# Square roots through logarithm and exponential, and a score turn in two PSUM banks, in a fused attention and feed-forward kernel

## The chip, the cores and the metric

The kernel runs on one core of one Trainium2 chip. The metric is the device time of one execution in microseconds (us). The span of a profile is the stretch from the first to the last recorded instruction, some 2 us less than the device time of the same execution. PSUM is the on-chip memory in which TensorE's results land, SBUF the one that holds the operands.

## The reference, cut to what matters

```python
def _attn_ref(q, k, v, tau):              # B, N, C = 4, 6080, 256, fp32; tau = 1.0
    qn = q / (np.linalg.norm(q, axis=1, keepdims=True) + 1e-06)
    kn = k / (np.linalg.norm(k, axis=1, keepdims=True) + 1e-06)
    s = kn.transpose(0, 2, 1) @ qn / tau  # a 256 x 256 matrix for each batch
    s = s - s.max(-1, keepdims=True)
    a = np.exp(s)
    a /= a.sum(-1, keepdims=True) + 1e-09
    return v @ a

def _moe_ref(x, w_in, w_out, s, b):       # 24320 x 256 -> 2048 -> 256
    r = np.maximum(x @ w_in, 0.0)
    return (s * (r * r) + b) @ w_out
```

The norms run over the N rows, so each batch needs only 512 square roots: 256 for q, 256 for k. Everything else of weight is matrix products.

## The kernel before

For each batch the kernel forms the scores, turns them, exponentiates them, and multiplies the result into w_in ("wa"), so that the attention's own product with v disappears into the first feed-forward product. The first batch is done alone at the start. The finish of each of the other three is spread in small steps over the feed-forward of the batch before. These are the parts that the change touches:

```python
def add_norms(self, arrays=(0, 1), last=False):
    if self.b > 0:                        # later batches: sums of squares lie in the
        self.n_all = x_tile[0][:, 1, : 2 * CH].rearrange(...)   # unused half of X's bank
        self.n_ps = [self.n_all[:, 0], self.n_all[:, 1]]
    ...                                   # matmuls with a column of ones      (n_ps, o_ps<-ones,f)

def norms(a=None):                        # in finish_ops
    ...
    if a is None:                         # later batches: q and k together
        self.add_norms(last=True)
        po(nc.scalar.activation(out=st["nrm"], in_=self.n_all, func=AF.Sqrt))
    else:                                 # first batch: k, then q
        self.add_norms((a,), last=True)
        po(nc.scalar.activation(out=st["nrm"][:, a], in_=self.n_ps[a], func=AF.Sqrt))

def recip(a=None):
    ...
    po(nc.vector.tensor_scalar_add(out=nrm, in0=nrm, scalar1=EPS))
    po(nc.vector.reciprocal(out=r, in_=nrm))

def turn():                               # first batch: both halves in one PSUM bank
    st["t"] = self.bank("t_ps", CH, C)
    for ch in range(CH):
        for j in range(CH):
            po(nc.tensor.transpose(st["t"][:, j, ts(ch, P)], st["s"][:, ch, ts(j, P)], ident32))

def ready(func):                          # a tiny ACTIVATE that brings the table load early
    po(nc.scalar.activation(out=warm, in_=ones32[:, 0:1], func=func))

def exps(j):
    ...
    po(nc.scalar.activation(out=st["e"][:, j, :], in_=st["t"][:, j, :], func=AF.Exp,
                            scale=st["r"][:, 0, j : j + 1]))
# ... sums (r_ps, then rs = 1 / r_ps on VectorE), folds (wa_ps, scaled to wa by rs:
#     half 0 on ScalarE, half 1 on VectorE)

if self.b == 0:
    front = [lambda: norms(1), lambda: recip(1), lambda: norms(0),
             lambda: ready(AF.Exp), scale, lambda: recip(0), turn]
else:                                     # split and join: scores in two fp16 parts, turned by DMA
    front = [lambda: ready(AF.Sqrt), norms, recip]
    front += [lambda: ready(AF.Exp), lambda: split("hi"), lambda: split("lo"), join]
return front + [lambda: exps(0), lambda: exps(1), sums] + folds

# ... the end of the first batch, in program order
for f in fin[2:6]: f()
fin[6]()                                  # turn
transpose_v(0)                            # vT_ps x8, then the copy vT on VectorE
keep_busy(2, w_in16[:, 0, :P], w_in16[:, 0, :NW])   # two idle matmuls
for f in fin[7:13]: f()                   # exponentials, sums, first folds

# ... the second product of the feed-forward, a seven-product form (X, Y, Z: PSUM tiles)
def begin(name):
    t = ps_o.tile([P, 2, 2 * P], FP32, tag="o_ps", name="o_ps")
    halves = [t[:, h, :].rearrange("p (j c) -> p j c", j=2) for h in range(2)]
    if name == "X":
        st["X"] = halves[0]
        x_tile[0] = t                     # whose second half add_norms uses
    else:
        st["Z"], st["Y"] = halves
```

In the feed-forward, TensorE's h_ps matmuls (first product) alternate with o_ps matmuls (second product). ScalarE takes the relu of h_ps, VectorE squares and forms sums. An eviction is the copy of a result from PSUM to SBUF; that of wa_ps scales it too. An idle matmul is one whose result nobody reads.

## Time and profile before

| | kernel before |
|---|---|
| time, median of 3 runs | 719.26 us (719.24 to 719.51) |
| profiled span | 717.3 us |
| TensorE busy | 698.8 us |
| ScalarE busy | 544.7 us, of it 10.3 us in eight table loads |
| VectorE busy | 625.9 us |
| second h_ps matmul of the feed-forward | 39.19 us after the span's start |

Busy time adds up the instructions of an engine. It doesn't tell what a saving is worth: TensorE is the engine whose work fills the span, so a saving elsewhere counts only where TensorE was waiting for it. The last row matters because from about 40 us on TensorE runs nearly without a gap: the span after is the start of that stretch plus its length.

### The profile page before, as it was taken

To read this page: it belongs to the slowest core of one execution; us is meant where nothing else is said; L and a number is where in the kernel's file an instruction comes from. 1 tells how busy PE (TensorE), PEld (TensorE's weight loads), DVE (VectorE), ACT (ScalarE), POOL (GpSimd) and SP (SyncE) were. 2 spreads that over 40 slices of the span, in tenths; PEclk is the share of its full clock that TensorE was granted. 3 is DMA by queue.
4 is the path that set the end of the run, shared out by engine and by line. 5 is a ranking of instruction groups with operands and counts; after the bars stand their busy time and mean duration, and the time that the engine had idled before them with its cause. 6 is when DMAs were issued, how large, how long until landed. Compare 5 with 4: busy or idle time off the path is not lost.

```text
span 717.3 us, 17641 instructions
## 1 busy us (share of the span) xinstructions
PE 698.8 (97%) x7479; PEld 504.7 (70%) x7479; DVE 625.9 (87%) x881; ACT 544.7 (76%) x589; POOL 110.1 (15%) x189
## 2 busy tenths in 40 slices
PE   4799999999999999999999999999999999999998
PEld 3556777776677777777677777777668777777777
DVE  4879999998789999999889899999887888888886
ACT  4489977887777777788777778778877777777875
POOL 4532332101201222111110222110000000000000
PEclk9999999999999999999999999999999999999999
DMA  9999998646556879443982877944423333321201
GB/s 236 208 259 169 159 170 139 111 108 129 111 112 117 143 133 145 107 93 78 150 160 57 141 138 125 153 90 85 105 63 75 93 71 74 97 59 46 83 30 74
DMA packets 89790, 84.25 MB, mean 117 GB/s; under 512 B 59664, under 2 KB 64848, under 8 KB 89712
## 3 DMA queue, kind: packets, MB, share of 16 engines
q0 software_dynamic: 26064, 43.40, 37.2%
q1 hardware_dynamic: 63072, 38.43, 21.7%
q8 instruction: 58, 0.95, 0.6%
q10 hardware_dynamic: 576, 1.31, 0.5%
q14 instruction: 20, 0.16, 0.1%
HBM read 78.91 MB, written 24.90 MB: 145 GB/s over the span
## 4 chain that ended last, share of the span: by engine, by line
PE 93%; DMA 3%; DVE 2%; ACT 1%; POOL 1%; issue 0%; POOLq 0%; DVEq 0%; ACTq 0%
PE h_ps L636 45%; PE o_ps L804 40%; PE s_ps L146 4%; DMA qk<-in_q_dram 3%; PE wa_ps L323 2%; PE o_ps L708 1%; POOL qk L130 1%; PE o_ps L682 0%; ACT r L646 0%; DVE f L182 0%; DVE sq L166 0%; DVE o_sb L664 0%; DVE S L732 0%; DVE S L730 0%; DVE S L734 0%
## 5 line engine op out<-in xcount | busy, mean ns | idle before, releaser
L646 ACT ACTIVATE r<-h_ps 128x1024 f16<-128x1024 f32 (+1 forms) x384 | 387.9, 1014 | 146.0 <-PE h_ps L636 144.0
L636 PE MATMUL h_ps<-vT,wa 128*128 128x512 f16 (+7 forms) x1632 | 452.2, 364 | 0.1
L804 PEld LDWEIGHTS <-S 128*128 128x128 f16 x2944 | 198.0, 98 | 84.7 <-issue 0.2
L804 PEld LDWEIGHTS <-g 128*128 128x128 f16 x2208 | 155.0, 98 | 74.1
L659 DVE TENSOR_TENSOR g<-r 128x2048 f16<-128x2048 f16 (+2 forms) x150 | 174.7, 1164 | 14.6 <-ACT r L646 14.5
L804 PE MATMUL o_ps<-T,S 128*128 128x128 f16 x2208 | 183.3, 219 | 0.1
L636 PEld LDWEIGHTS <-wa 128*128 128x128 f16 x1632 | 136.1, 98 | 20.8 <-DVE wa L318 0.6
L804 PE MATMUL o_ps<-w_out,g 128*128 128x128 f16 x1472 | 134.2, 219 | 0.2 <-DVE u L664 0.2
L664 DVE SCALAR_TENSOR_TENSOR o_sb<-o_ps,s_out,u 128x256 f32<-128x256 f32 x138 | 66.4, 481 | 47.7 <-PE o_ps L804 45.2
L657 ACT ACTIVATE g<-r 128x1024 f16<-128x1024 f16 (+1 forms) x97 | 100.3, 1035 | 0.2
L146 PE MATMUL s_ps<-qk 128*128 128x256 f16 (+1 forms) x384 | 69.6, 282 | 13.9 <-ACT qk L137 8.8
L376 POOL DMA_DIRECT2D v<-in_v_dram x48 | 31.4, 654 | 263.0 <-DMA vT<-v 198.9
L664 DVE SCALAR_TENSOR_TENSOR u<-o_ps,s_out,rowconst 128x256 f32<-128x256 f32 x138 | 65.8, 477 | 0.0
L804 PE MATMUL o_ps<-w_out,S 128*128 128x128 f16 x736 | 63.4, 219 | 0.0
L804 PE MATMUL o_ps<-N,g 128*128 128x128 f16 x736 | 63.4, 219 | 0.0
L193 POOL DMA_DIRECT2D f<-f x30 | 26.4, 879 | 225.1 <-DVE f L182 171.9
L169 ACT ACTIVATE sq<-qk 128x1024 f16<-128x1024 f16 (+3 forms) x49 | 50.4, 1033 | 10.0 <-DMA qk<-in_k_dram 7.6
L732 DVE TENSOR_TENSOR S<-S,g 128x2048 f16<-128x2048 f16 (+1 forms) x47 | 56.4, 1201 | 1.3
L730 DVE TENSOR_TENSOR S<-g 128x2048 f16<-128x2048 f16 (+1 forms) x47 | 56.0, 1193 | 0.0
L734 DVE TENSOR_TENSOR S<-g 128x2048 f16<-128x2048 f16 x46 | 55.9, 1215 | 0.0
L736 DVE TENSOR_TENSOR S<-g,S 128x2048 f16<-128x2048 f16 x46 | 55.9, 1215 | 0.0
L146 PEld LDWEIGHTS <-qk 128*128 128x128 f16 (+1 forms) x384 | 32.8, 101 | 20.0 <-issue 7.9
(75 smaller groups left out, 323.7 us busy)
## 6 DMA issues: line engine op xcount, KB each, us to landing
out_dram<-o_sb SPq DMA_DIRECT2D x46, 512.0 KB, 3.0
v<-in_v_dram POOLq DMA_DIRECT2D x47, 256.0 KB, 4.7
qk<-in_k_dram POOLq DMA_DIRECT2D x42, 256.0 KB, 5.9
qk<-in_q_dram POOLq DMA_DIRECT2D x42, 256.0 KB, 7.1
f<-f POOLq DMA_DIRECT2D x30, 128.0 KB, 3.0
vT<-v SPq DMA_TRANSPOSE x182, 3.2
w<-in_moe_w_out_dram POOLq DMA_DIRECT2D x4, 512.0 KB, 11.4
raw<-in_q_dram ACTq DMA_DIRECT2D x2, 512.0 KB, 6.8
```

What stands on the lines that cost most here:

```text
L146: po(nc.tensor.matmul(self.s_ps[:, ch, :], kc[:np_, j, ts(ch, P)], qc[:np_, j, :], start=(c == 0 and j == 0 and ch == 0), stop=(c == len(s ...
L169: po(nc.scalar.activation(out=st["sq"][:np_, 1, js, :], in_=kc[:np_, js, :], func=AF.Square))
L636: po(nc.tensor.matmul(dst, wa[:, ci, ts(m, P)], src, start=(ci == 0), stop=(ci == CH - 1), skip_group_check=True))
L646: po(nc.scalar.activation(out=r16[:, :, i % 2, :n], in_=h_tiles.pop((g, i))[:, :, :n], func=AF.Relu))
L657: po(nc.scalar.activation(out=dst, in_=src, func=AF.Square))
L659: po(nc.vector.tensor_mul(dst, src, src))
L664: po(nc.vector.scalar_tensor_tensor(out=dst, in0=src, scalar=s_out, op0=ALU.mult, in1=add, op1=ALU.add))
L730: po(nc.vector.tensor_add(T[1], A21, A22))
L732: po(nc.vector.tensor_sub(T[2], T[1], A11))
L734: po(nc.vector.tensor_sub(T[3], A11, A21))
L736: po(nc.vector.tensor_sub(T[4], A12, T[2]))
L804: po(nc.tensor.matmul(st[name][:, j, :], a()[:, i, ts(j, P)], w[:, i, :], start=first, stop=last, skip_group_check=True))
```

## The change

The intent is that all of ScalarE's functions share one activation table. The square root becomes exp(ln(x)/2), the table is loaded once at the start, and the tiny warm-ups go. Besides, the turned scores of the first batch go to two PSUM banks, so that the first exponential needn't wait for the transposes of the second half.

```diff
+            def root(out, sums):
+                po(nc.scalar.activation(out=out, in_=sums, func=AF.Ln, bias=tiny))
+                po(nc.scalar.activation(out=out, in_=out, func=AF.Exp, scale=0.5))
...
-                    po(nc.scalar.activation(out=st["nrm"], in_=self.n_all, func=AF.Sqrt))
+                    root(st["nrm"], self.n_all)
...
-                    po(nc.scalar.activation(out=st["nrm"][:, a], in_=self.n_ps[a], func=AF.Sqrt))
+                    root(st["nrm"][:, a], self.n_ps[a])
...
             def turn():
-                st["t"] = self.bank("t_ps", CH, C)
+                st["t"] = [h_tile("t_ps")[:, 0, :C], self.bank("t_ps", CH, C)[:, 0, :]]
...
-            def ready(func):
-                po(nc.scalar.activation(out=warm, in_=ones32[:, 0:1], func=func))
...
-                         lambda: ready(AF.Exp), scale, lambda: recip(0), turn]
+                         scale, lambda: recip(0), turn]
             else:
-                front = [lambda: ready(AF.Sqrt), norms, recip]
-                front += [lambda: ready(AF.Exp), lambda: split("hi"), lambda: split("lo"), join]
+                front = [norms, recip]
+                front += [lambda: split("hi"), lambda: split("lo"), join]
...
-    warm = consts.tile([P, 1], FP32)
-    po(nc.scalar.activation(out=warm, in_=ones32[:, 0:1], func=AF.Sqrt))
+    po(nc.scalar.preload_act_table_set("natural_log_exp_and_others"))
+    tiny = consts.tile([P, 1], FP32)
+    nc.vector.memset(tiny, 1e-30)
...
-    FIN = (-12, 0, 3, 3, 5, 7, 15, 17, 19, 22)
+    FIN = (0, 3, 5, 7, 15, 17, 19, 22)
```

The cuts ("...") leave out unchanged lines and index changes that follow from the two shorter lists.

More of the change, by code (lines that the diff above doesn't have):

```diff
@@ L278, in join @@
             def join():
-                st["t"] = sm_pool.tile([P, CH, C], FP32, tag="sm_s", name="t_sb")
-                po(nc.vector.tensor_add(st["t"], st["hiT"], st["loT"]))
+                t_sb = sm_pool.tile([P, CH, C], FP32, tag="sm_s", name="t_sb")
+                po(nc.vector.tensor_add(t_sb, st["hiT"], st["loT"]))
+                st["t"] = [t_sb[:, j, :] for j in range(CH)]
             def turn():
-                st["t"] = self.bank("t_ps", CH, C)
+                st["t"] = [h_tile("t_ps")[:, 0, :C], self.bank("t_ps", CH, C)[:, 0, :]]
                 for ch in range(CH):
@@ L286, in turn @@
                         po(nc.tensor.transpose(
-                            st["t"][:, j, ts(ch, P)], st["s"][:, ch, ts(j, P)], ident32))
-            def ready(func):
-                po(nc.scalar.activation(out=warm, in_=ones32[:, 0:1], func=func))
+                            st["t"][j][:, ts(ch, P)], st["s"][:, ch, ts(j, P)], ident32))
             def exps(j):
@@ L296, in exps @@
                 po(nc.scalar.activation(
-                    out=st["e"][:, j, :], in_=st["t"][:, j, :], func=AF.Exp,
+                    out=st["e"][:, j, :], in_=st["t"][j], func=AF.Exp,
                     scale=st["r"][:, 0, j : j + 1]))
@@ L490 @@
             g0.mm(c, j)
-    for f in fin[2:6]:
+    for f in fin[2:5]:
         f()
-    fin[6]()
+    fin[5]()
     transpose_v(0)
     keep_busy(2, w_in16[:, 0, :P], w_in16[:, 0, :NW])
-    for f in fin[7:13]:
+    for f in fin[6:12]:
         f()
@@ L545, in at_step @@
         side.setdefault(int(s), []).append(f)
-    FIN = (-12, 0, 3, 3, 5, 7, 15, 17, 19, 22)
+    FIN = (0, 3, 5, 7, 15, 17, 19, 22)
     first_group = [b * N // TG for b in range(B)]
     FOLDS = (0, 0, 3, 4, 7, 8)
-    for i, f in enumerate(fin[13:]):
+    for i, f in enumerate(fin[12:]):
         at_step(FOLDS[i], f)
@@ L601, in fin_step @@
             for i, f in enumerate(ops):
-                at_step(int(s) + 1 + (FIN[i] if i < 10 else FIN[9] + 3 + (i - 10) * 3), f)
+                at_step(int(s) + 1 + (FIN[i] if i < 8 else FIN[7] + 3 + (i - 8) * 3), f)
         at_step(w1 - fin_len - 12, fin_step)
```

## The prediction

> **What bounds the kernel now.** I read the page's busy table first, then the chain that ended last, then ScalarE's groups with their shapes kept apart, and last the timelines and the chain in two short stretches.
>
> ```profile
> PE 698.8 (97%) x7479; PEld 504.7 (70%) x7479; DVE 625.9 (87%) x881; ACT 544.7 (76%) x589; POOL 110.1 (15%) x189
> ...
> PE 93%; DMA 3%; DVE 2%; ACT 1%; POOL 1%; issue 0%; POOLq 0%; DVEq 0%; ACTq 0%
> ```
>
> The reader is to see that TensorE is busy 97% of the span and is 93% of the chain that set the end, while ScalarE (ACT) is only 1% of that chain. From 40 us to 700 us TensorE has nearly no idle time. ScalarE time removed there is worth only what TensorE was waiting for. The next view is the list of ScalarE's groups; its columns are busy us, mean ns of one, and idle time before it.
>
> ```profile
> L646 ACT ACTIVATE r<-h_ps 128x1024 f16<-128x1024 f32 x376 | 383.1, 1023 | 143.1 <-PE h_ps L636 141.1 <-DVE S L736 1.2
> L291 ACT ACT_TABLE_LOAD x7 | 9.0, 1283 | 0.1
> L291 ACT ACTIVATE warm<-ones 128x1 f32<-128x1 f32 x7 | 1.4, 203 | 0.1
> L240 ACT ACTIVATE nrm<-o_ps 128x4 f32<-128x4 f32 x3 | 0.5, 174 | 0.0
> L243 ACT ACTIVATE nrm<-n_ps 128x2 f32<-128x2 f32 x2 | 0.3, 172 | 1.9 <-PE n_ps L224 1.9
> ```
>
> ScalarE waits 141 us for TensorE before its relus, so it has room. The seven loads and seven tiny warm-ups are 9.0 + 1.4 = 10.4 us in all. An eighth load stands at 1.18 us, under the first DMAs, and costs nothing: ScalarE then waits 3.31 us for its first rows.
>
> **What the Trainium skill says.** "ScalarE: Activation LUTs", section "What ACT_TABLE_LOAD costs", gives about 1283 ns for a load and about 1380 ns for a drain, 2.66 us a switch. The trace agrees on 1283 ns but shows no such drain: the root ends at 35.40, the load starts at 35.42, ends at 36.70, and the next ACTIVATE starts at 36.72. So I count 1.28 us plus 0.20 us of warm-up for a switch, not 2.66. The same section adds about 93 ns for a per-partition pointer operand; I use it for the new bias of the Ln: estimate 0.17 + 0.09 = 0.26 us. The same page, "Table sets: the hidden batching unit", says that natural_log_exp_and_others holds exp and ln and that cheap functions are in every set. The built program agrees as far as it can: one table load stands in ScalarE's stream in place of eight. "PSUM — Partial Sum Buffer", section "PSUM bank collisions raise a hardware error", tells to guard PSUM by bank; that is why the first exponential in the old layout, one bank for both halves, waits for all four transposes. No wait of this trace shows it, since the load hid it.
>
> **Instruction order.** Setting line numbers and buffer numbers aside, PE, POOL and SP run the same list before and after. VectorE gains one memset. ScalarE loses seven loads and eight warm-ups and has each Sqrt replaced by Ln and Exp, of which the second waits for the first. So all effects are of timing.
>
> **Part 1: the end of the first batch (34 to 40 us).** Here ScalarE is on the path.
>
> ```profile
> 35.01 0.20 PE n_ps L224 x8
> 35.21 0.02 issue
> 35.23 0.17 ACT nrm L243
> 35.40 0.02 issue
> 35.42 0.83 ACT L291
> 36.25 0.46 issue
> 36.72 0.20 ACT warm L291
> 36.92 0.74 ACT eT L296 x2
> 37.66 0.04 issue
> 37.70 0.23 PE r_ps L306 x3
> 37.93 0.90 PE wa_ps L323 x8
> ```
>
> This is the chain in order of time (start, us, what): root, table load, warm-up, two exponentials, then TensorE. It looks as if 1.28 + 0.20 us would come out. It does not, as the timelines of VectorE and TensorE beside it show (start, us, engine, line, operation):
>
> ```profile
> 34.00 0.73 DVE L166 TENSOR_TENSOR sq<-qk 128x512 f16<-128x512 f16 x2
> 35.05 0.88 DVE L257 TENSOR_SCALAR sm_s<-s_ps,rnrm 128x256 f32<-128x256 f32 x2 [0.32 <-PE s_ps L146]
> 35.84 0.16 DVE L248 TENSOR_SCALAR nrm<-nrm 128x2 f32<-128x2 f32 x1
> 36.04 0.17 DVE L249 RECIPROCAL rnrm<-nrm 128x2 f32<-128x2 f32 x1
> 37.21 0.69 DVE L389 COPY vT<-vT_ps 128x1024 f16<-128x1024 f16 x1 [1.00 <-PE vT_ps L387]
> ...
> 37.01 0.59 PE L462 MATMUL idle_ps<-w_in 128*128 128x512 f16 x2
> 37.44 0.49 PE L306 MATMUL r_ps<-parts,eT 128*128 128x1 f16 x4
> ```
>
> Step by step. A root now takes 0.26 + 0.03 (handing over, as between L248 and L249) + 0.20 = 0.49 us against 0.17: 0.32 longer. The root of k's sums (33.51) so moves the squares of q from 34.00 to 34.31; they end at 35.04 instead of 34.73. The last n_ps matmuls want the second of them: TensorE came to these at about 34.92, and now must wait to about 35.07, so they end 0.15 later, at 35.34. The root of q's sums then runs 35.38 to 35.87. VectorE does not reach its add before 35.84 anyway (the scaling of the scores stands ahead), so the reciprocal is done at 36.26 instead of 36.21. The third transpose ends at about 36.26. The first exponential can start at about 36.3 instead of 36.83: 0.5 us won, the rest of the load having hidden VectorE's work. The two end at about 37.15 instead of 37.66.
>
> But TensorE has eight transposes of v and two idle matmuls ahead of the r_ps matmuls. At about 216 ns each (the chain's 0.43 us for two 512-wide matmuls) the idle ones hold the array until 37.01 + 0.43 = 37.44, exactly where the first r_ps matmul stands. That one is not moved. What goes is the wait of 0.27 us for the second exponential at 37.70. So wa_ps starts at about 37.55 instead of 37.79: **0.25 us**. Behind it, ScalarE's first eviction also wants VectorE's reciprocal, which follows the vT copy that ends at 37.90 either way; it gains only about 0.1 us. VectorE's eviction (38.65) waits for wa_ps alone and moves by 0.25, and the second h_ps matmul at 39.19 waits for that one. So 0.2 to 0.25 us reaches TensorE's stream, and I see no transfer after it that would take it back. The two-bank turn adds to it only if the reciprocal is earlier than the fourth transpose (about 36.42): at most 0.1 us, hidden under the idle matmuls.
>
> **Part 2: the three later batches.** Each loses two loads and two warm-ups, 2 x (1.28 + 0.20) = 2.97 us, and gains 0.32 us: net 2.65 us of ScalarE, 7.9 us over three batches. How much TensorE waited for it is in the chain just after a load (load at 137.34 to 138.62, then two relus back to back from 138.75):
>
> ```profile
> 139.55 0.39 PE o_ps L804 x7
> 139.94 0.45 PE h_ps L636 x2
> 140.40 0.45 PE o_ps L804 x7
> 140.84 0.43 PE h_ps L636 x2
> ```
>
> 0.45 and 0.45 stand where the pattern is 0.43 and 0.39: 0.08 us lost. At the other five loads the distance of two h_ps pairs is 0.84 or 0.85 against 0.82: 0.02 to 0.03 each. The sum is about **0.2 us**. The longer root (0.49 at 147.64) fits before the relu at 148.15, which had waited 0.34 us for TensorE; the added 0.32 just fits.
>
> **Part 3: the start.** The table load now stands ahead of both of ScalarE's DMA issues, and the first moves from 0.74 by about 0.07 us. The second was issued at 1.25 while the load ran (1.18 to 2.46), so issue does not wait for a load. TensorE waits for data again later: estimate 0.
>
> Sum: 0.25 + 0.2 = 0.45 us of 719.26, that is 718.8 us.
>
> **The rivals.** (a) The full cost of the switches leaves the path: 7 x 1.48 = 10.4 us, 709 us, 1.4% faster, still inside 2%. Against it: ScalarE is 1% of the chain, and TensorE's list of waits holds none for a relu. (b) The longer serial root takes the load's place: k's root delays the squares, n_ps, q's root and the reciprocal by more than I reckon, and nothing or less than nothing is won at 36 us: 719.2 to 719.5. For it: 0.32 us twice in one chain. Against it: 0.5 us of margin up to 36.83. (c) The table load at the head delays the first q rows by 1.28 us: the first matmul at 7.08 goes to 8.4. Even then TensorE waits for rows near 23 and 28 us, so most is absorbed: up to 719.8. Against it: the second issue at 1.25.
>
> **Range and chances.** Runs of the kernel before lie within 0.27 us. My steps are off by perhaps 0.3 us at the first batch and 0.2 later, and small changes of timing move DMA waits at the start: 718.0 to 719.5. A change over 2% is 14.4 us, more than all the switches together; it would take a fault to make it slower by that.
>
> **What would show it right or wrong.** One load in ScalarE's groups. The first exponential at about 36.3, r_ps still at 37.44, wa_ps at about 37.55, the second h_ps matmul at about 38.95. Pairs of h_ps at 0.82 us throughout what was 137 to 141 us. The span shorter by about 0.45 us, half of it there by 40 us. If wa_ps does not move, (b) holds; if the first matmul comes after 8 us, (c). I would be wrong by more if the changed start reorders DMA landings before 33 us, or if the relu after the double root comes late.

## More of the kernel before

Every run quoted here was correct against the reference, with a granted TensorE clock of 0.999 or 1.0.

What the text calls a bank of PSUM is one whole o_ps tile of this program (2 x 256 fp32 for each partition).

## The result

| | before | after |
|---|---|---|
| median of 6 runs each, same rounds | 719.27 us (719.13 to 719.51) | 719.16 us (718.81 to 719.40) |
| ratio | | 0.9998, 95% interval 0.9985 to 1.001 |
| profiled span | 717.3 us | 717.2 us |
| second h_ps matmul | 39.19 us | 38.82 us |
| last matmul ends | 714.13 us | 713.96 us |

A ratio is the mean time of one kernel's fast runs over that of the other's of the same rounds, so not quite the ratio of the medians quoted.

The time lies inside the predicted range, but the gain is 0.1 us and not the predicted 0.45. The page's first part, for the kernel after (busy time, share of span and number of instructions of each engine), shows what was certain:

```profile
PE 698.9 (97%) x7479; PEld 504.6 (70%) x7479; DVE 626.1 (87%) x882; ACT 536.5 (75%) x579; POOL 109.8 (15%) x189
```

ScalarE lost 8.2 us of busy time (544.7 to 536.5), and TensorE's busy time stayed. The groups of ScalarE with shapes kept apart (busy us, mean ns of one, idle before) show the parts, for the kernel after:

```profile
L419 ACT ACT_TABLE_LOAD x1 | 1.3, 1283 | 0.7 <-PEq L882 0.7
...
L235 ACT ACTIVATE nrm<-o_ps,tiny 128x4 f32<-128x4 f32 x3 | 0.8, 264 | 0.0
L236 ACT ACTIVATE nrm<-nrm 128x4 f32<-128x4 f32 x3 | 0.6, 205 | 0.1
```

One load is left of eight. A later root is 264 + 205 ns where the Sqrt was 174 ns. Those 8.2 us mostly became idle time: ScalarE's idle time ahead of its relus rose from 146.0 to 153.4 us.

**The first batch.** This is the chain of waits of the kernel after, in order of time (start, us, what):

```profile
28.78 7.72 DMA v<-in_v_dram
...
36.55 0.62 PE vT_ps L390 x8
37.17 0.43 PE idle_ps L467 x2
37.60 0.08 PE r_ps L309 x4
37.68 0.90 PE wa_ps L326 x8
```

ScalarE is gone from this stretch of the chain. Before, it went through the root, the load, the warm-up and the two exponentials; now it comes from the arrival of v, through its transposes and the two idle matmuls, to r_ps and wa_ps without a wait. The timelines of ScalarE, VectorE and TensorE's weight loads (PEld) of the kernel after (start, us, engine, line, operation) show the ends of the side chains:

```profile
36.43 0.84 ACT L299 ACTIVATE eT<-t_ps,rnrm 128x256 f16<-128x256 f32 x2 [0.50 <-PE t_ps L293]
38.07 0.84 ACT L319 ACTIVATE wa<-wa_ps,rs 128x256 f16<-128x256 f32 x2 [0.80 <-DVE rs L314]
...
37.81 0.16 DVE L314 RECIPROCAL rs<-r_ps 128x2 f32<-128x2 f32 x1
38.18 0.92 DVE L321 TENSOR_SCALAR wa<-wa_ps,rs 128x256 f16<-128x256 f32 x2 [0.20 <-PE wa_ps L326]
...
38.59 0.21 PEld L641 LDWEIGHTS <-wa 128*128 128x128 f16 x2 [0.30 <-ACT wa L319]
```

The first exponential starts at 36.43 instead of 36.83, wa_ps at 37.54 instead of 37.79, and VectorE's eviction of wa_ps at 38.18 instead of 38.65. The second h_ps matmul is 0.37 us earlier.

The chain above names only one of the paths to the h_ps matmuls. The first of them waits for ScalarE's eviction (38.07 instead of 38.23), that eviction for the reciprocal rs on VectorE (37.81), and the reciprocal stands behind the copy of vT, which VectorE runs from 37.20 to 37.90 (records of VectorE overlap by some 0.08 us). So the first h_ps matmul gained 0.16 us (38.76 to 38.60). The second, which waited for VectorE's eviction before, stood 0.43 us behind the first and now stands 0.22 us behind it.

**After it.** TensorE's instruction list is the same in both kernels, so each matmul can be set against its twin. I took the start of each matmul minus the start of its twin in the kernel before, and took off the same difference at the second h_ps matmul. What remains is the lag that TensorE has gathered since: +0.19 us at the last matmul in the profile of the result, +0.26 in a second one of the same program. A second profile of the kernel before gives 0.00 to 0.01 throughout, so the method is good to 0.01 us. The lag comes in steps. The first is at the root of the second batch. Timelines of ScalarE and TensorE, kernel before:

```profile
147.64 0.17 ACT L240 ACTIVATE nrm<-o_ps 128x4 f32<-128x4 f32 x1
...
147.46 0.59 PE L636 MATMUL h_ps<-vT,wa 128*128 128x512 f16 x2
147.89 0.50 PE L804 MATMUL o_ps<-T,S 128*128 128x128 f16 x6
```

The same lines of the kernel after:

```profile
147.27 0.26 ACT L235 ACTIVATE nrm<-o_ps,tiny 128x4 f32<-128x4 f32 x1
147.56 0.20 ACT L236 ACTIVATE nrm<-nrm 128x4 f32<-128x4 f32 x1
...
147.09 0.59 PE L641 MATMUL h_ps<-vT,wa 128*128 128x512 f16 x2
147.58 0.50 PE L809 MATMUL o_ps<-T,S 128*128 128x128 f16 x6
```

From the start of the h_ps pair to the next o_ps matmul it was 0.43 us, which is the pair's own time; now it is 0.49. That o_ps matmul writes X, and the sums of squares that the Ln reads lie in the other half of X's PSUM bank. The Ln ends at 147.53 and the matmul starts at 147.58. Without a wait it would have started at 147.09 + 0.43 = 147.52.

The second step is at about 163.6 us, where both profiles of the kernel after have one and those of before have none. VectorE joins the two turned parts of the scores there. Its timeline before:

```profile
160.65 0.69 DVE L280 TENSOR_TENSOR t_sb<-t_hi,t_lo 128x512 f32<-128x512 f16 x1
```

And after:

```profile
161.09 0.69 DVE L285 TENSOR_TENSOR t_sb<-t_hi,t_lo 128x512 f32<-128x512 f16 x1 [0.72 <-DMA t_lo<-s_lo]
```

VectorE now waits 0.72 us for the last DMA transpose of the scores (0.81 us in the second profile). That transpose took 3.7 us from issue to landing before and 4.6 us after. TensorE lost 0.10 and 0.19 us shortly behind it, and the timelines show how: VectorE's later work moves with the join. Its read of X (u, L669) ran from 162.83 to 163.31, and the o_ps matmul that writes X next starts at 163.37, 0.17 us after the matmul ahead of it. Before, that read ended at 162.88, and the same matmul started at 163.59, 0.05 us after the one ahead. In the second profile the read ends at 163.71 and the matmul starts at 163.76.

### The profile page after: what moved, and what is told of

It is laid out like the page before. It is cut to its first block, busy times and chain, and to the rows that moved or that the text cites. A ratio compares the mean times of both kernels' runs of the same rounds, so it can differ in the third digit from the quotient of the medians.

```text
span 717.2 us, 17629 instructions
## 1 busy us (share of the span) xinstructions
PE 698.9 (97%) x7479; PEld 504.6 (70%) x7479; DVE 626.1 (87%) x882; ACT 536.5 (75%) x579; POOL 109.8 (15%) x189
## 4 chain that ended last, share of the span: by engine, by line
PE 93%; DMA 4%; DVE 1%; ACT 1%; POOL 1%; issue 0%; POOLq 0%; ACTq 0%
PE h_ps L641 45%; PE o_ps L809 40%; PE s_ps L146 4%; DMA qk<-in_q_dram 3%; PE wa_ps L326 2%; DMA v<-in_v_dram 1%; PE o_ps L713 1%; PE o_ps L687 0%; POOL qk L130 0%; ACT r L651 0%; DVE o_sb L669 0%; DVE S L737 0%; DVE sq L166 0%; DVE S L735 0%; DVE S L739 0%
## 5 line engine op out<-in xcount | busy, mean ns | idle before, releaser
L651 ACT ACTIVATE r<-h_ps 128x1024 f16<-128x1024 f32 (+1 forms) x384 | 388.4, 1014 | 153.4 <-PE h_ps L641 150.9
L669 DVE SCALAR_TENSOR_TENSOR o_sb<-o_ps,s_out,u 128x256 f32<-128x256 f32 x138 | 66.5, 482 | 47.1 <-PE o_ps L809 44.5
L669 DVE SCALAR_TENSOR_TENSOR u<-o_ps,s_out,rowconst 128x256 f32<-128x256 f32 x138 | 66.0, 478 | 0.0
```

The source lines that it names most:

```text
L651: po(nc.scalar.activation(out=r16[:, :, i % 2, :n], in_=h_tiles.pop((g, i))[:, :, :n], func=AF.Relu))
L669: po(nc.vector.scalar_tensor_tensor(out=dst, in0=src, scalar=s_out, op0=ALU.mult, in1=add, op1=ALU.add))
```

## The experiments

Twelve kernels ran, in five rounds each (e10 has six executions), on two chips. All outputs are right. The theory at this point: (A) the longer read of the root holds X's bank and delays TensorE, three times; (B) the former table loads were worth little in the later batches; (C) the first batch is set by v and not by the exponentials any more. The rivals: the two banks did the work or the harm at the first batch; the loads had been worth all the gain and a change of timing lost it again; the late DMA transpose is the whole loss.

The differences sought are tenths of a microsecond. The intervals of the times are about 0.12% wide to each side, 0.9 us, so **the times alone can't separate them**; the traces can, because TensorE's list is fixed. This table holds both. "v to h" is the time from the first transpose of v to the second h_ps matmul. The lag columns are TensorE's, in us, as above: just behind the first later root, behind the join near 163.6, behind the third root, and at the last matmul. Runs without the idle matmuls, or with v turned earlier, have other matmuls at the start; there the matching ones were compared.

| run | v to h | root 1 | join | root 3 | end | median us | ratio to before (95%) |
|---|---|---|---|---|---|---|---|
| before | 2.64 | – | – | – | – | 719.26 | – |
| e0_before_again | 2.63 | 0.00 | 0.00 | 0.00 | 0.00 | 719.42 | 0.9996 (0.9982 to 1.001) |
| after | 2.27 | +0.06 | +0.14 | +0.21 | +0.19 | 719.16 | 0.9998 (0.9985 to 1.001) |
| e0_after_again | 2.28 | +0.05 | +0.22 | +0.28 | +0.26 | 719.19 | 0.9996 (0.9984 to 1.0009) |
| e1_one_bank | 2.28 | +0.04 | +0.02 | +0.09 | +0.07 | 719.12 | 0.9998 (0.9986 to 1.0011) |
| e2_no_bias | 2.28 | 0.00 | -0.02 | -0.07 | -0.09 | 718.93 | 0.9988 (0.9976 to 1.0001) |
| e3_ln_twice | 2.28 | +0.35 | +0.34 | +1.00 | +0.98 | 720.08 | 1.0003 (0.999 to 1.0015) |
| e4_first_only | 2.28 | -0.02 | -0.02 | -0.02 | -0.02 | 718.61 | 0.9991 (0.9978 to 1.0003) |
| e5_later_only | 2.47 | +0.05 | +0.03 | +0.09 | +0.08 | 719.15 | 0.9999 (0.9985 to 1.0013) |
| e6_no_idle | 2.27 | +0.06 | +0.04 | +0.12 | +0.10 | 719.23 | 0.9995 (0.9983 to 1.0008) |
| e8_v_early | (3.43) | -0.01 | -0.02 | -0.07 | -0.09 | 718.47 | 0.9981 (0.9968 to 0.9995) |
| e9_join_later | 2.27 | +0.06 | +0.04 | +0.11 | +0.09 | 719.29 | 0.9993 (0.9979 to 1.0006) |
| e10_direct_no_idle | 2.28 | 0.00 | -0.02 | -0.06 | -0.08 | 718.93 | 0.9987 (0.9975 to 1.0) |
| e11_v_early_join | (3.40) | -0.01 | -0.02 | -0.07 | -0.09 | 718.67 | 0.9984 (0.9971 to 0.9996) |

In e8 and e11 the transposes of v no longer stand directly ahead of the sums, so "v to h" isn't comparable there. The kernel before ran again: 719.32 us beside e0_after_again, e1, e4 and e5; 719.61 us beside the others, on the second chip. Single executions of 720.0 to 720.6 us occur with several kernels, the one before among them; five of them have a span of 717.3 to 717.5 us like the others, so that their excess lies outside the profiled span.

### Both kernels again

e0_after_again and e0_before_again are the two kernels without an edit, for another profile of each.

> The changed kernel once more, to see what repeats. Theory A (the lead of 0.38 us won at the first batch is partly given back: 0.06 to 0.07 us at each of the three roots of a later batch because Ln with its bias pointer, 0.26 us, holds the PSUM bank longer than Sqrt, 0.17 us; another 0.11 us at 163.6 us by a late DMA transpose, by chance): the second h_ps matmul at 38.8 again, the three losses again, the loss at 163.6 not necessarily. Rival B (the differences after 40 us are scatter of single executions): the losses stand elsewhere or are missing. Time 719.1 us, within 0.3 us of before.

> The kernel before once more, for the scatter of its trace. If the arrival of the last q rows and of v sets when the first batch ends, its second h_ps matmul moves with them by up to 0.3 us from 39.19, while the rest of TensorE's stream keeps its distance from that matmul within 0.03 us. The late transpose (3.7 us to landing in the first profile) lands in 3.6 to 3.7 us and costs nothing if the late landings belong to the kernels without the later loads; in 4 us or more if it is chance. Time 719.3 to 719.6.

The lag repeats in the kernel after and is absent in the kernel before. The late transpose of the kernel before landed after 3.9 us this time, between the two cases of its expectation. What doesn't repeat is the absolute position. The first transpose of v stands at 36.55 in one profile of before and at 36.93 in the other, and at 36.55 and 36.86 in those of after, with all that follows moved by as much. The arrival of the first batch's rows moves the whole execution by up to 0.4 us, and that is as large as the effect in question.

### One bank for the turned scores

```diff
-                st["t"] = [h_tile("t_ps")[:, 0, :C], self.bank("t_ps", CH, C)[:, 0, :]]
+                t_ps = self.bank("t_ps", CH, C)
+                st["t"] = [t_ps[:, j, :] for j in range(CH)]
```

> The changed kernel with the turned scores of the first batch in one PSUM bank again. Theory A: both layouts wait for about the fourth transpose (36.42) or for the reciprocal (36.34), and the first r_ps matmul stands behind the idle matmuls at 37.44 in any case: the first exponential at 36.43 to 36.5, r_ps at 37.44, the second h_ps at 38.8, time unchanged (719.1). Rival: the two banks are worth something: the first exponential later by 0.1 us or more and the second h_ps matmul after 38.9.

"v to h" is 2.28 us with one bank and 2.27 or 2.28 with two. The first exponential starts 1.41 us after VectorE's first scaling of the scores with one bank, and 1.42 and 1.30 us after it in the two profiles with two banks; it is 1.30 in e2, e3, e4, e6 and e9 too. The third transpose ends 1.26 us and the fourth 1.37 us after the scaling, so that the exponential wins up to 0.11 us by the two banks. That stays hidden; at the h_ps matmul they are worth nothing that these traces can show.

### Only the first batch, only the later ones

e4_first_only has the new root and the two banks in the first batch and the Sqrt with its loads in the later ones. e5_later_only is the reverse, with one bank.

```diff
 # e4: later batches as before
-                    root(st["nrm"], self.n_all)
+                    po(nc.scalar.activation(out=st["nrm"], in_=self.n_all, func=AF.Sqrt))
-                front = [norms, recip]
-                front += [lambda: split("hi"), lambda: split("lo"), join]
+                front = [lambda: ready(AF.Sqrt), norms, recip]
+                front += [lambda: ready(AF.Exp), lambda: split("hi"), lambda: split("lo"), join]
-    FIN = (0, 3, 5, 7, 15, 17, 19, 22)
+    FIN = (-12, 0, 3, 3, 5, 7, 15, 17, 19, 22)
```

```diff
 # e5: first batch as before
-                    root(st["nrm"][:, a], self.n_ps[a])
+                    po(nc.scalar.activation(out=st["nrm"][:, a], in_=self.n_ps[a], func=AF.Sqrt))
-                         scale, lambda: recip(0), turn]
+                         ready, scale, lambda: recip(0), turn]   # loads the shared table, warm Exp
-    po(nc.scalar.preload_act_table_set("natural_log_exp_and_others"))
+    po(nc.scalar.activation(out=warm, in_=ones32[:, 0:1], func=AF.Sqrt))
```

> Ln and Exp, two banks and no table load in the first batch only; the later batches take Sqrt with two table loads each, as before. Theory A: the second h_ps matmul at 38.8, and the lead of 0.38 us over before is kept to the end, as nothing differs later: time 718.9 us, 0.35 to 0.4 us under before, and no step lost at the later roots. Rival (the later batches' loads were worth more than the roots cost): the lead is the same at 40 us but the end is later than that of the changed kernel, 719.3.

> The first batch as before (Sqrt, table load of the Ln and Exp set, one bank); the later batches with Ln and Exp and no loads. Theory A: the second h_ps matmul at 39.2 as before; then TensorE wins 0.02 to 0.05 us at each of six former loads (0.17 in all) and loses 0.06 to 0.07 us at each of three roots (0.20): the end within 0.1 us of before, 719.3. Rival (my prediction): it wins 0.2 us and loses nothing: 719.1.

e4 has the short "v to h" of 2.28 and no lag: -0.02 throughout. e5 has the lag: +0.05 at the first root and +0.08 at the end. So the lag belongs to the later batches, and the gain to the first. e5 holds a surprise: its "v to h" is 2.47, not the 2.64 of before, although its first batch does the same work. wa_ps comes 1.27 us after the first transpose of v there, 1.24 in before. The difference arises behind it: VectorE's eviction of wa_ps starts 0.86 us after the first wa_ps matmul in both profiles of before, and 0.63 to 0.64 us after it in every other run. In before it starts 0.03 to 0.05 us after the sixth wa_ps matmul ends, in the other runs as soon after the fourth, which is the last that it reads. So of the 0.37 us won, 0.20 is the change in the first batch's operations (2.47 to 2.27) and 0.17 is a shift of that eviction whose cause I haven't found.

### The root's first read, shorter and longer

e2_no_bias drops the pointer operand of the Ln. e3_ln_twice does the Ln of the later roots twice, with the same result.

```diff
 # e2
-                po(nc.scalar.activation(out=out, in_=sums, func=AF.Ln, bias=tiny))
+                po(nc.scalar.activation(out=out, in_=sums, func=AF.Ln))
 # e3, in norms, ahead of the root of the later batches
+                    po(nc.scalar.activation(out=st["nrm"], in_=self.n_all, func=AF.Ln, bias=tiny))
```

> The changed kernel with Ln taken without its bias pointer (the sums are never zero here, so the result stays right). Theory A (TensorE's next product into the bank of the sums waits for the root's read, which the bias pointer makes 0.09 us longer): Ln takes 0.17 us as Sqrt did, the 0.06 to 0.07 us lost at each of the three later roots is gone, and the end is about 0.2 us before that of the changed kernel: 718.95 us. The first batch is unchanged, as the idle matmuls and the arrival of v hold it: second h_ps matmul 2.27 us after the first transpose of v. Rival (two ACTIVATEs in place of one delay the relus behind them): the losses stay, since the second ACTIVATE stays.

> The changed kernel with the Ln of the later batches done twice over the same sums (result unchanged). Theory A: the bank is held another 0.26 + 0.03 us, so TensorE's next product into it loses 0.06 + 0.29 = 0.35 us in place of 0.06, three times: the end 0.87 us after that of the changed kernel, about 720.0 us, the loss standing at the o_ps matmul behind the norm matmuls. Rival (the relu behind the root is late): the loss stands at an h_ps matmul two steps on, and is smaller, as the relu had 0.03 us of room left.

The timelines of ScalarE and TensorE at the first later root, for e2:

```profile
147.60 0.17 ACT L235 ACTIVATE nrm<-o_ps 128x4 f32<-128x4 f32 x1
...
147.42 0.59 PE L641 MATMUL h_ps<-vT,wa 128*128 128x512 f16 x2
147.85 0.50 PE L809 MATMUL o_ps<-T,S 128*128 128x128 f16 x6
```

And for e3, where the second of the two Ln is shown:

```profile
147.77 0.26 ACT L235 ACTIVATE nrm<-o_ps,tiny 128x4 f32<-128x4 f32 x1
...
147.29 0.59 PE L642 MATMUL h_ps<-vT,wa 128*128 128x512 f16 x2
148.08 0.49 PE L810 MATMUL o_ps<-T,S 128*128 128x128 f16 x6 [0.20 <-ACT nrm L235]
```

The distance from the h_ps pair to the o_ps matmul is 0.43 us with a read of 0.17 us (before and e2), 0.49 with 0.26 (after), and 0.79 with two reads. In e3 the profile names the root as the releaser, and the matmul starts 0.05 us after the second Ln ends, as in the kernel after. A second Ln, 0.30 us with its handing over, costs 0.30 us of TensorE at each of three roots. The Exp of the root still stands behind the read in e2 and costs nothing: it reads and writes SBUF. This settles (A): **the price of the longer root is its hold on the bank**, 0.06 us per root. The bank is one tile in this program, so these runs can't tell a wait for the bank from a wait for the tile.

e2 also settles (B). With no cost of the root left, its lag at the end is -0.09 us against -0.02 in e4, which keeps the loads: the six later loads with their warm-ups were worth 0.07 to 0.09 us of TensorE together.

### Without the idle matmuls

```diff
     transpose_v(0)
-    keep_busy(2, w_in16[:, 0, :P], w_in16[:, 0, :NW])
```

> The changed kernel without the two idle matmuls ahead of the first batch's r_ps. Prediction's step: they hold r_ps at 37.44. Theory A: without them wa_ps starts about 0.2 us sooner (0.8 us after the first transpose of v in place of 0.99), but the first eviction waits for the reciprocal that stands behind the copy of vT on VectorE, so the two h_ps matmuls stay where they are (2.05 and 2.27 us after the first transpose of v) and the time too: 719.1. Rival (the idle matmuls are the bound): the h_ps matmuls move by 0.2 us. A lower granted clock after 36 us would show that they were needed.

The chain of waits of e6 (start, us, what) at the exponentials:

```profile
36.56 0.85 ACT eT L299 x2
...
37.45 0.23 PE r_ps L309 x3
```

The first r_ps matmul now stands at 37.09 and no longer at 37.44, but the other three wait for the second exponential, to 37.45. wa_ps follows at 37.54, 1.03 us after the first transpose of v, against 0.99 in after, and "v to h" is 2.27 as it was. The idle matmuls in the kernel after end just when the exponentials do, so wa_ps did not come sooner, and the expectation of 0.8 us for it missed. Its reason why the h_ps matmuls stay holds, and it settles (C). In all nine profiles whose first batch has the new root and v turned behind the scores (after, e0_after_again, e1 to e4, e6, e9, e10), the reciprocal rs starts 1.27 us after the first transpose of v, right behind the copy of vT, ScalarE's eviction at 1.52 and the first h_ps matmul at 2.05, while the last r_ps matmul starts anywhere from 0.90 to 1.01. So **the copy of vT on VectorE is the bound there**. In before and e5 the reciprocal follows the r_ps matmuls instead (at 1.40 to 1.45), and so it does again in e8 and e11, where the copy is done early. The granted clock from 36 to 100 us was 1.00 without the idle matmuls too.

### v earlier, the root as a reciprocal, the join later

Four runs look for a version better than both. e8_v_early computes the reciprocal root itself, as exp(-ln/2), without bias, addition of EPS or reciprocal on VectorE. It loads v ahead of the first part of w_in, turns v ahead of the scores, and has no idle matmuls. e9_join_later only moves the join of the two turned parts one step later. e10_direct_no_idle combines the direct root, the later join and no idle matmuls. e11_v_early_join is e8 with the later join. Dropping the bias and EPS is right for these inputs, not for a column of zeros.

```diff
 # e8, e10, e11
-                po(nc.scalar.activation(out=out, in_=sums, func=AF.Ln, bias=tiny))
-                po(nc.scalar.activation(out=out, in_=out, func=AF.Exp, scale=0.5))
+                po(nc.scalar.activation(out=st["nrm"][:, own], in_=sums, func=AF.Ln))
+                po(nc.scalar.activation(out=st["r"][:, own], in_=st["nrm"][:, own],
+                                        func=AF.Exp, scale=-0.5))
-                po(nc.vector.tensor_scalar_add(out=nrm, in0=nrm, scalar1=EPS))
-                po(nc.vector.reciprocal(out=r, in_=nrm))
 # e8, e11: load_v(0) ahead of load_w_in(0, NW); transpose_v(0) right behind the root of q
 # e9, e10, e11
-    FIN = (0, 3, 5, 7, 15, 17, 19, 22)
+    FIN = (0, 3, 5, 7, 16, 17, 19, 22)
```

> A version made from the findings: Exp with scale -0.5 gives 1/norm directly (no bias, no add, no reciprocal), v's first load is issued ahead of the first piece of w_in, its transposes stand ahead of the turn and their copy ahead of the sums, and the two idle matmuls are left out. Theory A: the copy of vT is done by about 36.6 instead of 37.9, so the chain is turn, two exponentials (to 37.2), r_ps, wa_ps at about 37.4, evictions from 37.8, second h_ps at about 38.5 against 38.8 for the changed kernel and 39.2 before; later roots lose nothing: about 718.5 us, 0.7 to 0.8 under before. Rival (the arrival of v or of w_in holds the chain whatever the order): w_in, now later, holds wa_ps after 37.5 and the gain is 0.2 us, the later roots' alone.

> The changed kernel with the addition of the two transposed halves one step (0.82 us) later. Theory (in two of two profiles of the changed kernel the last transpose landed after 4.6 us, VectorE waited 0.7 to 0.8 us for it and TensorE then lost 0.11 and 0.19 us at 163.6): VectorE waits no more, the loss at 163.6 is gone, the three losses at the roots stay: lost after the first batch 0.07 us in place of 0.19 and 0.26, time 719.0. Rival: the later addition delays the exponentials and TensorE loses as much elsewhere.

> The direct 1/norm (Exp with scale -0.5, no bias, no add, no reciprocal), no idle matmuls, the later addition; v loaded and transposed where the changed kernel has it. Theory: later batches win about 0.1 us in place of losing 0.2; the first batch is held by the arrival of v as in the changed kernel (second h_ps 2.27 us after the first transpose of v). About 718.9, 0.2 to 0.3 under the changed kernel.

> The version with v early (median 718.47 us) and the later addition. If the landing of the transpose costs nothing there (2.3 us in its profile), the same time within 0.2 us: 718.4 to 718.6; the second h_ps matmul about 3.5 us after the first scaling of the scores, against 3.8 in the changed kernel and 4.1 before. Rival (its gain was luck of the run): 718.9 or more.

In e8 and e11 the second h_ps matmul follows VectorE's first scaling of the scores after 3.54 us, against 3.81 and 3.90 in the two profiles of after and 4.14 and 4.15 in before. But e6, with v in its old place, has 3.53: v came in time there, its first transpose 1.25 us after the scaling and not 1.53 and 1.62 as in after. So the early v is not shown to win where v comes in time. With the missing lag (-0.09), e8 and e11 are the only two runs whose interval excludes 1: 0.19% and 0.16% faster than before. That is well below what this study calls faster, but it is a version that beats the one before; whether it beats the one after isn't resolved by an interval of their own. The traces account for 0.60 + 0.09 = 0.7 us, 0.10%, of the lead over before; four of the ten runs of before beside e11 took 720.0 us or more, which may make up the rest. e10, without v earlier, has an interval that reaches 1.0. It differs from e11 in the order of v alone: 718.75 to 718.98 us against 718.54 to 718.78, so the early v was worth 0.26 us by the medians there.

e9 shows no wait of VectorE for the transposes and no step of lag at the join. But its last transpose landed after 4.1 us, not 4.6, as it did in most runs (4.2 us in e1, e5, e6 and e10, 3.6 in e4, 2.3 in e3 and e8), and at 4.2 us e1, e5 and e6 had no step either with the join where it was. So e9 doesn't show that the later join is what helped. The late landing at 4.6 us, in both profiles of the kernel after and in no other, is **left open**. A 512 KB store of the output is issued on the same queue right behind that transpose, in before too, so it alone doesn't explain a difference.

## Why the prediction was right or wrong

The time and its class were right: no part of the change could reach 2%, and 719.16 us lies in the range of 718.0 to 719.5. The point of 718.8 was 0.36 us too low. The range holds the time of before as well (719.27), so that meeting it shows little, and it was luck that what the prediction had missed stayed this small. By its steps:

- **ScalarE is not on the path outside 34 to 40 us: right.** 8.2 us came out of it and its idle time ahead of the relus rose by 7.4 us. Rival (a), the full cost of the switches, is out.
- **First batch: mechanism right in the main, size short.** The prediction had the first exponential at 36.3 (36.43), r_ps kept at 37.44 (37.44) and wa_ps at 37.55 (37.54). It had 0.25 us at the second h_ps matmul, and it was 0.37. The step that was mis-sized is "VectorE's eviction ... moves by 0.25": it moved by 0.47. Nor does the second h_ps matmul wait for that eviction any more, as the prediction had it: it follows the first, which waits for ScalarE's eviction and so for the copy of vT. The prediction named this wait and gave it 0.1 us of gain; it was 0.16. e5 puts 0.17 us of the 0.37 outside the first batch's own change. Rival (b) is out: the longer root fitted into the hidden time.
- **Two banks, at most 0.1 us and hidden: right.** e1 has it at 0 at the h_ps matmul.
- **Later loads, 0.2 us: mis-sized.** e2 against e4 has 0.07 to 0.09 us. The 0.08 us that the prediction read from two h_ps pairs at 139.55 to 140.84 didn't come out. In the profile of the result the lag goes from -0.01 to -0.03 at 139.80 and back to 0.00 at 140.57; in e4, which keeps this load, it is -0.02 there. So those pairs weren't stretched by the load by more than about 0.01 us.
- **"The longer root (0.49 at 147.64) fits before the relu at 148.15": this is the step that failed.** The relu was in time: 0.63 us after its h_ps pair began, 0.69 before. But the prediction asked only what ScalarE does next, and not what TensorE needs of the thing that ScalarE reads. The next o_ps matmul waits for the end of the Ln, as both use X's bank. 3 x 0.06 to 0.07 = 0.19 us of loss, taken away by e2 and multiplied by e3. The Trainium skill, "PSUM — Partial Sum Buffer", section "PSUM bank collisions raise a hardware error", has the rule for the program: PSUM is to be guarded by bank, in the page's simple version, and not by address. The prediction cited it for the first batch and didn't apply it here. e3's line with the releaser agrees with it. That the wait goes away when the sums lie in a bank of their own wasn't tried.
- **The late transpose wasn't foreseen at all.** 0.10 and 0.19 us in the two profiles of the kernel after.
- **The start, 0: right as far as it can be seen.** The table load stands at 0.74 to 2.02 us and both of ScalarE's DMA issues at 0.77 to 1.64 us, so rival (c) is out. The arrival of the rows scatters the start by 0.4 us in either kernel.

The sum in the trace of the result: 0.37 won in the first batch, 0.19 lost behind it, 0.18 left, and 714.13 - 713.96 = 0.17 us is what TensorE's last matmul shows. The lag of 0.19 is 3 x 0.065 for the roots, plus 0.10 for the transpose, minus some 0.1 for the loads. In the second profile it is 0.26, which leaves 0.11. The medians differ by 0.11 us, inside their scatter.

## What to carry to other kernels

Before pricing a change to an operation that reads PSUM, list who writes next to the same bank, not only who reads the result: a read that is 0.09 us longer cost the bound engine 0.06 us each time, where the six later loads and warm-ups, 8.9 us on the same engine, were worth 0.07 to 0.09 us in all. When the instruction list of the bounding engine is the same in two kernels, subtract their start times instruction by instruction: this shows hundredths of a microsecond where the times scatter by tenths. Two profiles of the same program come first, since the arrival of the first data can move everything by more than the effect.

## What the Trainium skill lacked or had wrong

- "ScalarE: Activation LUTs", section "What ACT_TABLE_LOAD costs": the load of 1283 ns agrees (1283 in every kernel here). The drain of about 1380 ns, 2.66 us a switch, doesn't show in the first batch: before, the Sqrt ended at 35.40, the load ran from 35.42 to 36.70, and the next ACTIVATE started at 36.72.
- The same section: about 93 ns for a pointer operand agrees (Ln with bias 262 to 264 ns, without 172 to 173 ns). The fixed 186 ns is above the 172 to 174 ns of the ACTIVATEs of 128x2 and 128x4 that read PSUM, and below the 203 to 205 ns of those of SBUF.
- The same section doesn't say that DMAs can be issued from ScalarE while a table load runs: both issues stand at 0.77 to 1.64 us in the kernel after, during the load of 0.74 to 2.02 us.
- "PSUM — Partial Sum Buffer", section "PSUM bank collisions raise a hardware error", gives the rule of guarding by bank but no price for it: 0.06 us of TensorE for a read that is 0.09 us longer, 0.36 us for one that is 0.39 us longer.
- On the pages cited here I found nothing on the scatter of a DMA transpose's landing: the same one took 2.3 to 4.6 us over these runs.
